# Attention sums in bursts over two shared PSUM banks, with a new order of work, in a four-layer transformer kernel

## The chip, the cores and the metric

One core of one Trainium2 chip. The metric is the device time of one execution in microseconds (us). All runs here are of one core, and "fast" here means within 1.5% of the fastest run of the same kernel. Engines: PE (matmuls), ACT (activations, here the exponentials), DVE (vector work), POOL, and SP (which here only starts DMAs).

## The reference, cut to what matters

The program is four residual layers: linear attention (A), softmax attention (B), A, B. The input has 2048 tokens of width 1024, 32 heads of 32.

```python
def _A_ref(x, wqkv, w_phi, wo):          # linear attention
    q, k, v = ...                        # x @ wqkv
    pq, pk = q @ w_phi, k @ w_phi        # per head
    phi_q = concat([softmax(pq), softmax(-pq)]); phi_k = ...
    kv = einsum("bhsf,bhsd->bhfd", phi_k, v)     # needs every token
    ...                                  # o = phi_q @ kv / den
    return o @ wo
def _B_ref(x, wqkv, wo):                 # softmax attention
    scores = einsum("bhqd,bhkd->bhqk", q, k) * Dh ** -0.5
    p = softmax(scores)
    return (p @ v) @ wo
x = A_x
x = x + _A_ref(layernorm(x), ...)
x = x + _B_ref(layernorm(x), ...)
x = x + _A_ref(layernorm(x), ...)
x = x + _B_ref(layernorm(x), ...)
```

Two things follow. The two softmax layers need 2 x 32 x 2048 x 2048 exponentials. And `kv` in layer A needs every token, so the second A layer can't finish before the first B layer has.

## The kernel before

The kernel is a program that writes a program: while it is built it keeps a clock of its own with a cost for each operation, and it decides from that clock which instruction comes next on each engine. The program that it writes has a fixed order on each engine. Attention is cut into 1024 steps, in the main of two heads x two tiles of 128 keys x 512 queries: 4 QK matmuls (row tiles), 2 exps of 128x1024, and for each exp a group of 4 matmuls of sums (column tiles: values and row sums of both heads). An E tile holds what one exp puts out until its sums have read it. A unit is a run of such steps that adds up in one bank. Everything else (projections with their blocks of weights, the "slabs", the A layers, norms) is "background": tasks that are slipped in between the steps, if their inputs and a PSUM bank are there.

The kernel divides PSUM into eight banks: six are three double-bank `ring` tiles for QK results, one (`acc`) is for sums, one (`bg`) for background.

```python
ring_t = [pps.tile([P, 2, C], F32, ...) for i in range(3)]
acc_t = pps.tile([P, C], F32, tag="acc", name="acc")
bg_t = pps.tile([P, C], F32, tag="bg", name="bg")
# ... cut ...
def exp_chain(u, kks, e, buf):
    E = yield ("take", e_s)                  # 5 E tiles
    yield ("op", "S", c_act(2 * n), lambda x: nc.scalar.activation(
        out=E[:, :, 0:n], in_=ring_t[buf][:, :, 0:n], func=ACT.Exp, scale=INV_SQRT_DH))
    ring.give(buf)
    sums.append((u, kks, e, E))

def emit_sums():                             # sums of an exp as soon as it is there
    while sums:
        u, kks, e, E = sums[0]
        if u.nsum == 0 and not acc_s.free:
            return
        sums.pop(0)
        if u.nsum == 0:
            u.acc = acc_s.take()             # held until the unit's last sum is added
        # ... cut: 4 matmuls into u.acc per 512 columns of E ...
        clk.at(st["t"], lambda E=E: e_s.give(E))
        if final:
            clk.start(finish_unit(u), st["t"] + PE_LAT)      # DVE takes acc out

def get_bank():                              # for a background task
    if bg_free[0]:
        bg_free[0] = False
        # ...
        return bg_t, rel
    if att_active():
        return None                          # ring halves only while no attention runs
    # ... cut: halves of the ring ...

while True:                                  # the order on PE
    # ... cut ...
    if ready and len(ring.free) >= 2:
        emit_step()                          # QK of the next step
        # ... cut ...
        emit_sums()
        continue
    # ... cut: sums, then one background matmul, then wait ...
```

In attention a background "matmul" of 128x512 is written as four column-tiled matmuls ("a group"), so that PE needn't change the tiling mode (row tiles for QK, column tiles for sums; in the trace, at full clock, a group after a group starts 0.216 us later, a QK after a group 0.322 us later); outside attention it is one full-width matmul.

The first layer's tiles are loaded and normalised only when the slot for their transposed chunk is free:

```python
def first_x():
    for t in range(NT):
        u = (0, "K", t // 4)
        yield ("key", ("xs", u))             # the slot
        xb = yield from grab(t_x)
        clk.start(first_x1(u, t, xb))        # load, statistics, normalise
```

The softmax here doesn't subtract the row's maximum and nothing guards it: scores larger than these inputs give would overflow.

Of the kernel before, what the change touches and what calls it, by code (L numbers as in the profile page):

```python
# [35 lines left out]
RATE = {"D": 200e3, "P": 150e3}  # L36
# [181 lines left out]
class Task:  # L218
# [18 lines left out]
    (0, 4, (0,), False, False, (0, 1)), (0, 4, (1,), True, False, (0, 1)), (0, 4, (0, 1), False, False, (2, 3)),  # L237
    (4, 4, (0, 1), False, False, (0, 1, 2, 3, 4, 5, 6, 7)), (0, 4, (0, 1), False, False, (6, 7)),
    (0, 4, (0, 1), False, False, (4, 5)), (8, 4, (0, 1, 2), False, False, (4, 5)),
    (8, 4, (0, 1, 2), False, False, (6, 7)), (0, 4, (2, 3), True, True, (0, 1, 2)),  # L240
    (0, 4, (2, 3), True, True, (3, 4, 5)), (0, 4, (2, 3), True, True, (6, 7)),
    (4, 4, (2, 3), True, True, (6, 7)), (4, 4, (2, 3), True, True, (0, 1, 2, 4, 5)),
    (8, 4, (3,), True, True, (4, 5)), (4, 4, (2, 3), True, True, (3,)),
    (8, 4, (0, 1, 2, 3), False, True, (0, 1)), (8, 4, (0, 1), False, False, (2, 3)),
    (8, 4, (2, 3), True, True, (2, 3)), (8, 4, (3,), True, True, (6, 7)),
    (12, 2, (0, 1, 2, 3), False, True, (6, 7)), (12, 2, (0, 1, 2, 3), False, True, (0, 1, 2, 3, 4, 5)),
    (14, 2, (0, 1, 2, 3), False, True, (0, 3, 6, 7)), (14, 2, (0, 1, 2, 3), False, True, (4, 5)),
    (14, 2, (0, 1, 2, 3), False, True, (1, 2)),
)
VIS3 = (  # L250
    (0, 4, (0,), False, False, (0, 1, 2, 3, 4, 5)), (0, 4, (0,), False, False, (6, 7)),
    (0, 4, (1,), True, False, (0, 1)), (0, 4, (1,), True, False, (2, 3)),
    (4, 4, (0, 1), False, False, (0, 1, 2, 3, 4, 5)), (0, 4, (1,), True, False, (4, 5)),
    (0, 4, (1,), True, False, (6, 7)), (4, 4, (0, 1), False, False, (6, 7)), (0, 4, (2,), True, False, (0, 1)),
    (8, 4, (0, 1, 2), False, False, (0, 1, 2, 3)), (0, 4, (2,), True, False, (2, 3)),
    (8, 4, (0, 1, 2), False, False, (4, 5, 6, 7)), (0, 4, (3,), True, True, (0, 1)),
    (0, 4, (3,), True, True, (2, 3)), (0, 4, (2,), True, False, (4, 5)), (4, 4, (2, 3), True, True, (2, 3)),
    (4, 4, (2, 3), True, True, (0, 1)), (0, 4, (2,), True, False, (6, 7)), (0, 4, (3,), True, True, (4, 5)),
    (0, 4, (3,), True, True, (6, 7)), (4, 4, (2, 3), True, True, (6, 7)), (4, 4, (2, 3), True, True, (4, 5)),
    (12, 2, (0, 1, 2, 3), False, True, (0, 1, 2, 3, 4, 5)), (14, 2, (0, 1, 2, 3), False, True, (1, 2, 4, 5)),  # L260
    (8, 4, (3,), True, True, (0, 1, 2, 3, 4, 5, 6, 7)), (14, 2, (0, 1, 2, 3), False, True, (3,)),
    (14, 2, (0, 1, 2, 3), False, True, (0,)), (12, 2, (0, 1, 2, 3), False, True, (6, 7)),
    (14, 2, (0, 1, 2, 3), False, True, (6, 7)),
# [4 lines left out]
    ('AK', 0, 1, (0, 1), (0,)), ('AK', 0, 0, (0,), (0,)), ('fold', ('pk', 1)), ('AK', 0, 2, (1,), (0,)),  # L268
    ('fold', ('pk', 0)), ('AK', 0, 1, (0, 1), (1,)), ('AO', 0, 0), ('fold', ('pq', 1)),
    ('AK', 0, 0, (0, 1), (1,)), ('AK', 0, 0, (1,), (0,)), ('DN', 0, 0), ('AK', 0, 2, (0,), (1,)),  # L270
    ('AK', 0, 2, (1,), (1,)), ('AK', 0, 3, (0,), (1,)), ('fold', ('pq', 0)), ('AK', 0, 2, (0,), (0,)),
    ('AK', 0, 3, (1,), (0,)), ('DN', 0, 1), ('AO', 0, 1), ('AK', 0, 3, (1,), (1,)), ('AK', 0, 3, (0,), (0,)),
    ('PQ', 0, 1), ('PQ', 0, 0), ('DN', 0, 2), ('PQ', 0, 2), ('BP', 1, 0, (0, 1, 2)), ('BP', 1, 1, (0, 1)),
    ('BP', 1, 2, (0, 1)), ('BP', 1, 1, (2, 3)), ('BP', 1, 0, (3,)), ('PQ', 0, 3), ('AO', 0, 2), ('DN', 0, 3),
    ('BP', 1, 2, (2,)), ('BP', 1, 2, (3,)), ('AO', 0, 3), ('BP', 1, 3, (0, 1)), ('BP', 1, 3, (2,)),
    ('BP', 1, 3, (3,)), ('AK', 2, 0, (0,), (0,)), ('AK', 2, 0, (1,), (0,)), ('BO', 1, 1, 4), ('BO', 1, 8, 10),
    ('PS', 2, 0), ('BO', 1, 11, 13), ('BO', 1, 4, 8), ('BO', 1, 10, 11), ('AK', 2, 1, (1,), (1,)),
    ('BO', 1, 0, 1), ('PS', 2, 1), ('AK', 2, 0, (0, 1), (1,)), ('AK', 2, 2, (0,), (0,)), ('BO', 1, 13, 15),
    ('AK', 2, 2, (1,), (0,)), ('PS', 2, 2), ('BO', 1, 15, 16), ('AK', 2, 1, (0, 1), (0,)),
    ('AK', 2, 1, (0,), (1,)), ('AK', 2, 3, (1,), (0,)), ('AK', 2, 2, (0,), (1,)), ('AO', 2, 0),  # L280
    ('AK', 2, 3, (0,), (0,)), ('AK', 2, 3, (0,), (1,)), ('DN', 2, 1), ('AK', 2, 2, (1,), (1,)),
    ('AK', 2, 3, (1,), (1,)), ('DN', 2, 0), ('PS', 2, 3), ('BP', 3, 0, (0, 1)), ('AO', 2, 1),
    ('BP', 3, 2, (0, 1)), ('AO', 2, 3), ('BP', 3, 0, (2, 3)), ('BP', 3, 2, (2,)), ('BP', 3, 1, (0, 1)),
    ('BP', 3, 2, (3,)), ('DN', 2, 2), ('BP', 3, 3, (0, 1)), ('BP', 3, 1, (2, 3)), ('BO', 3, 12, 14),
    ('AO', 2, 2), ('BO', 3, 15, 16), ('BO', 3, 6, 10), ('DN', 2, 3), ('BO', 3, 14, 15), ('BO', 3, 11, 12),
    ('BO', 3, 0, 2), ('BP', 3, 3, (3,)), ('BP', 3, 3, (2,)), ('BO', 3, 2, 6), ('BO', 3, 10, 11),
# [3 lines left out]
class Unit:  # L290
    def __init__(self, l, vi, qt, w, ks, p, part, last):
        self.l, self.vi, self.qt, self.w, self.ks, self.p = l, vi, qt, w, ks, p
        self.q = qt // 4
        self.n = w * P
        self.g, self.b = divmod(p, 2)
        self.part, self.last = part, last
        kk = [2 * c + m for c in ks for m in range(2)]
        per = 4 // w
        self.steps = [tuple(kk[i:i + per]) for i in range(0, len(kk), per)]
        self.nsum = 0  # L300
        self.acc = None
        self.Q = None
        self.fast = False
# [3 lines left out]
def kernel(  # L307
# [71 lines left out]
    t_x, t_xn, t_phi, t_eq, t_o, t_oT = tok(4), tok(3), tok(8), tok(8), tok(4), tok(4)  # L379
# [4 lines left out]
    acc_t = pps.tile([P, C], F32, tag="acc", name="acc")  # L384
    bg_t = pps.tile([P, C], F32, tag="bg", name="bg")
    ring = Slots(clk, [0, 1, 2])
    acc_s = Slots(clk, [acc_t])
    bg_free = [True]
# [15 lines left out]
    def queue(q, kb):  # L404
        def lat():
            qbusy[q] = max(qbusy[q], clk.now) + kb * 1024 / RATE[q]
            return qbusy[q] - clk.now + DMA_LAT
        return lat
# [7 lines left out]
    def dma_t(o, i):  # L416
        return ("op", "D", 1.3, lambda e: nc.sync.dma_start_transpose(out=o, in_=i), queue("D", 400))
# [123 lines left out]
    def first_x():  # L541
        for t in range(NT):
            u = (0, "K", t // 4)
            yield ("key", ("xs", u))
            xb = yield from grab(t_x)
            clk.start(first_x1(u, t, xb))
# [67 lines left out]
    def slab_plan():  # L614
        want = sorted((slab_next(s), s) for s in slab_use)
        for nxt, s in want[:12]:
            if nxt >= 1 << 30:
                break
# [565 lines left out]
    def finish_unit(u):  # L1184
        token = t_acc
        n = u.n
        if u.part:
            yield ("key", ("pl", u))
            b = part_b.pop(u)
            token = t_part  # L1190
            a = b[:].bitcast(F32)[:, 0:n]
            yield tt("V", c_ps(n), a, a, acc_t[:, 0:n], ALU.add)
        else:
            b = yield from grab(t_acc)
            a = b[:].bitcast(F32)[:, 0:n]
            yield ("op", "V", c_ps(n), lambda e: nc.vector.tensor_copy(out=a, in_=acc_t[:, 0:n]))  # L1196
        acc_s.give(acc_t)
# [132 lines left out]
    sums = []  # L1330
    halves = []
# [65 lines left out]
    def emit_sums():  # L1397
        while sums:
            u, kks, e, E = sums[0]
            if u.nsum == 0 and not acc_s.free:  # L1400
                return
            sums.pop(0)
            if u.nsum == 0:
                u.acc = acc_s.take()
            set_mode("col")
            n = u.n
            n0, d0 = 64 * u.b, 64 * (1 - u.b)
            for i, kk in enumerate(kks):
                c, m = divmod(kk, 2)
                first = u.nsum == 0  # L1410
                u.nsum += 1
                final = u.nsum == 4 * len(u.ks)
                for r0, ld in ((n0, None), (d0, ones)):
                    for j in range(2):
                        h = 2 * u.p + j
                        lh = Vc[c][h // 16][:, 2 * m + e, DH * (h % 16):DH * (h % 16 + 1)] if ld is None else ones[:]
                        nc.tensor.matmul(  # L1417
                            u.acc[r0 + 32 * j:r0 + 32 * j + 32, 0:n], lhsT=lh, rhs=E[:, j, i * n:(i + 1) * n],
                            start=first, stop=final, tile_position=(0, r0 + 32 * j), skip_group_check=True)
                st["t"] += MM * n / C  # L1420
# [150 lines left out]
```

## Time and profile before

| | before |
|---|---|
| time, median of 4 | 2466.0 us |
| profiled span | 2464.0 us |
| ACT busy | 2121 us, 86% |
| exps (2048, starting 904 ns apart in the median) | at least 1851 us |
| time outside attention (before the first exp, gaps of over 2.5 us between exps, after the last) | 517 us |
| attention (the rest) | 1947 us |

The page of the kernel before, its second part: each digit is one of 40 equal slices (61.6 us), the busy share of ACT in tenths, and the granted PE clock in tenths of full speed.

```profile
ACT  4542279996999999999997438999999999999997
PEclk9999999999998899999999999999999995886579
```

ACT is full in two long stretches, the two B layers; where it is not, something else has to be done first. The PE clock is low late in the second.

The same trace by stage (each row a stretch; busy us of each engine and its instructions, PE clock, DMA share, GB/s). The stretches end where exps begin or stop:

```profile
core 0: us, PE busy (x) PEld busy (x) DVE busy (x) ACT busy (x) POOL busy (x), PEclk, DMA share, GB/s
0.00:336.10 336.10, 282.65 (x1983) 151.82 (x1987) 221.30 (x441) 133.21 (x242) 84.61 (x126) 0.98 0.53 161
336.10:578.80 242.70, 231.49 (x3396) 87.68 (x3392) 92.75 (x184) 242.02 (x272) 8.88 (x12) 1.00 0.40 125
578.80:602.90 24.10, 19.40 (x176) 11.72 (x177) 16.18 (x36) 6.02 (x15) 6.37 (x9) 0.93 0.20 53
602.90:1337.70 734.80, 682.68 (x10923) 278.60 (x10915) 420.73 (x674) 728.79 (x816) 127.68 (x141) 0.97 0.35 108
1337.70:1479.40 141.70, 121.50 (x843) 61.89 (x843) 99.59 (x211) 57.17 (x103) 27.15 (x37) 0.99 0.51 146
1479.40:2451.50 972.10, 890.90 (x12231) 325.46 (x12228) 420.54 (x739) 953.90 (x1045) 133.99 (x142) 0.87 0.36 113
2451.50:2464.00 12.50, 7.59 (x40) 3.09 (x39) 5.34 (x7) 0.00 (x0) 0.00 (x0) 0.98 0.11 42
```

Read it like this: rows 2, 4 and 6 are attention with ACT at 98 to 100%. Rows 1, 3, 5 and 7 are the time in which ACT mostly has nothing to do, and in rows 1, 3 and 5 PE works 80 to 86% of the time: what bounds them is projection work on PE and the chains of latency in it. So a change can win by moving background from rows 1, 3 and 5 under the exps, and it can lose by keeping ACT waiting in the others.

And the costliest groups of instructions, from the page: exps, sums, and QK, with the idle time before them:

```profile
L1361 ACT ACTIVATE E<-ring 128x1024 bf16<-128x1024 f32 x2048 | 1905.3, 1183 | 24.8 <-PE ring L1381 24.4
L1417 PE MATMUL acc<-E,V 128*32 128x512 bf16 (+1 forms) x5120 | 694.6, 372 | 2.8 <-ACT E L1361 2.1
...
L1381 PE MATMUL ring<-Q,K2b 32*128 32x512 bf16 (+1 forms) x2560 | 433.0, 364 | 118.2 <-ACT E L1361 110.6
```

PE waited 118 us ahead of one half of the QKs, 111 us of it for an exp to free its ring tile. That is spare time of PE in attention.

### The profile page before, as it was taken

What the parts mean: (1) busy time and instruction counts of PE and PEld (TensorE: products, weight loads), DVE (VectorE), ACT (ScalarE), POOL (GpSimd) and SP (SyncE); (2) the same over time, 40 slices, a digit from 0 to 9 for tenths busy, and PEclk for the clock granted to TensorE, in tenths of its full rate; (3) what the DMA queues carried; (4) which work ended last, traced back from release to release, by engine and by line L of the source; (5) the groups of instructions that cost most, each with busy time, mean ns of one, the idle gap of its engine ahead of it and who ended that gap; (6) DMA issues with size and microseconds to landing.
All of it is one profiled execution on the core that took longest, in us unless ns stands there. A gap on an engine that the chain in (4) does not pass through costs nothing.

```text
span 2464.0 us, 68772 instructions
## 1 busy us (share of the span) xinstructions
PE 2236.2 (91%) x29569; PEld 920.3 (37%) x29569; DVE 1276.4 (52%) x2289; ACT 2121.1 (86%) x2488; POOL 388.7 (16%) x465
## 2 busy tenths in 40 slices
PE   6898899999998989999989889899999989988997
PEld 3444343334332223334444443333333331243233
DVE  6787543244345566476566764534343555432453
ACT  4542279996999999999997438999999999999997
POOL 3321100001011212121114110100020122111120
PEclk9999999999998899999999999999999995886579
DMA  6553563343533332232235445436535353200111
GB/s 223 190 168 83 129 180 108 117 128 106 164 121 121 95 104 89 99 120 52 88 96 189 123 125 159 147 108 195 180 128 149 125 181 124 91 28 19 58 56 40
DMA packets 209906, 296.03 MB, mean 120 GB/s; under 512 B 94656, under 2 KB 113088, under 8 KB 206528
## 3 DMA queue, kind: packets, MB, share of 16 engines
q1 hardware_dynamic: 184512, 185.72, 25.5%
q0 software_dynamic: 25088, 105.92, 12.9%
q8 instruction: 231, 3.78, 0.6%
q14 instruction: 75, 0.61, 0.1%
HBM read 191.95 MB, written 79.69 MB: 110 GB/s over the span
## 4 chain that ended last, share of the span: by engine, by line
PE 46%; ACT 20%; issue 6%; DVE 4%; DMA 1%; ACTq 0%; POOL 0%; DVEq 0%; POOLq 0%
ACT E L1361 18%; PE bg L446 14%; PE acc L1417 14%; PE ring L1381 13%; PE ring L449 3%; DVE blk L432 1%; PE bg L449 1%; DMA xnT<-blk 1%; ACT blk L758 1%; DVE blk L1230 0%; ACT blk L919 0%; DVE blk L1223 0%; DVE sm L799 0%; DMA kvacc<-blk 0%; PE ring L988 0%
## 5 line engine op out<-in xcount | busy, mean ns | idle before, releaser
L1361 ACT ACTIVATE E<-ring 128x1024 bf16<-128x1024 f32 x2048 | 1905.3, 1183 | 24.8 <-PE ring L1381 24.4
L1417 PE MATMUL acc<-E,V 128*32 128x512 bf16 (+1 forms) x5120 | 694.6, 372 | 2.8 <-ACT E L1361 2.1
L1417 PE MATMUL acc<-E,ones 128*32 128x512 bf16 (+1 forms) x5120 | 694.4, 372 | 0.0
L1381 PE MATMUL ring<-Q,K2b 32*128 32x512 bf16 (+1 forms) x2560 | 433.0, 364 | 118.2 <-ACT E L1361 110.6
L1381 PE MATMUL ring<-Q,K2a 32*128 32x512 bf16 (+1 forms) x2560 | 451.7, 366 | 8.5 <-ACT E L1361 8.2
L1417 PEld LDWEIGHTS <-V 128*32 128x32 bf16 x5120 | 199.9, 99 | 298.5 <-issue 271.8
L432 POOL TENSOR_TENSOR blk<-blk,blk 64x512 bf16<-64x512 f32 (+1 forms) x156 | 169.3, 1085 | 713.5 <-DVE blk L1230 573.9
L1381 PEld LDWEIGHTS <-K2a 32*128 32x128 bf16 x2560 | 120.3, 92 | 411.9 <-issue 404.4
L1381 PEld LDWEIGHTS <-K2b 32*128 32x128 bf16 x2560 | 158.9, 92 | 249.5 <-issue 240.1
L1196 DVE COPY blk<-acc 128x512 f32<-128x512 f32 (+1 forms) x160 | 93.3, 583 | 271.9 <-PE acc L1417 271.3
L1230 DVE RECIPROCAL blk<-blk 128x128 f32<-128x128 f32 x252 | 223.8, 923 | 1.8
L1417 PEld LDWEIGHTS <-ones 128*32 128x32 bf16 x5120 | 197.6, 99 | 2.0
L446 PE MATMUL bg<-xnT,slab 128*32 128x512 bf16 x2912 | 192.7, 382 | 5.8 <-DVE K2b L427 2.1
L432 DVE TENSOR_TENSOR blk<-blk,acc 128x512 f32<-128x512 f32 x128 | 87.4, 683 | 172.6 <-PE acc L1417 169.5
L446 PE MATMUL bg<-slab,blk 128*32 128x512 bf16 x2560 | 171.6, 386 | 0.5
L446 PE MATMUL bg<-slab,xnT 128*32 128x512 bf16 (+1 forms) x2496 | 150.2, 361 | 1.6 <-DVE blk L755 0.6
L446 PEld LDWEIGHTS <-slab 128*32 128x32 bf16 x3688 | 101.2, 97 | 104.3 <-issue 21.3
L432 DVE TENSOR_TENSOR blk<-blk,bg 128x512 bf16<-128x512 bf16 x103 | 70.4, 684 | 117.0 <-PE bg L446 113.7
L758 ACT ACTIVATE blk<-ring 128x512 bf16<-128x512 f32 x84 | 47.3, 597 | 97.1 <-PE ring L449 75.9
L449 PEld LDWEIGHTS <-xnT 128*128 128x128 bf16 x792 | 76.8, 98 | 107.4 <-issue 25.7
L427 DVE CAST blk<-bg 128x512 bf16<-128x512 f32 x74 | 51.0, 690 | 123.6 <-PE bg L446 115.9
L446 PEld LDWEIGHTS <-blk 128*32 128x32 bf16 x2904 | 80.2, 98 | 68.9 <-issue 11.8
(184 smaller groups left out, 2281.3 us busy)
## 6 DMA issues: line engine op xcount, KB each, us to landing
slab<-in_B_wqkv_dram POOLq DMA_DIRECT2D x33, 1024.0 KB, 6.6
pd<-blk SPq DMA_DIRECT2D x128, 256.0 KB, 2.3
blk<-pd SPq DMA_DIRECT2D x128, 256.0 KB, 3.5
Q<-qd SPq DMA_DIRECT2D x112, 256.0 KB, 2.8
qd<-blk SPq DMA_DIRECT2D x64, 256.0 KB, 2.6
x<-blk SPq DMA_DIRECT2D x48, 256.0 KB, 2.1
blk<-x SPq DMA_DIRECT2D x48, 256.0 KB, 4.0
slab<-in_A_wqkv_dram POOLq DMA_DIRECT2D x9, 1024.0 KB, 6.6
```

Of the source, the lines that this page charges most:

```text
L427: eng(e).tensor_copy(out=o, in_=i)
L432: return ("op", e, cost, lambda x: eng(x).tensor_tensor(out=o, in0=a, in1=b, op=op))
L446: nc.tensor.matmul(o[js], lhsT=l[:, js], rhs=r, start=st, stop=sp, tile_position=(0, 32 * j), skip_group_check=True)
L449: nc.tensor.matmul(o, lhsT=l, rhs=r, start=st, stop=sp, skip_group_check=True)
L758: yield ("op", "S", c_act(C), lambda x, s=s: nc.scalar.activation(out=e[:, s * C:(s + 1) * C], in_=src, func=ACT.Exp, scale=1.0 - 2.0 * s))
L1196: yield ("op", "V", c_ps(n), lambda e: nc.vector.tensor_copy(out=a, in_=acc_t[:, 0:n]))
L1230: yield ("op", "V", 0.06 + 0.0063 * P, lambda e, x=x: nc.vector.reciprocal(out=r[:, x:x + P], in_=r[:, x:x + P]))
L1361: yield ("op", "S", c_act(2 * n), lambda x: nc.scalar.activation(out=E[:, :, 0:n], in_=ring_t[buf][:, :, 0:n], func=ACT.Exp, scale=INV_SQR ...
L1381: nc.tensor.matmul(ring_t[bufs[e]][:, j, i * n:(i + 1) * n], lhsT=K2[e][c][u.g // 4][r, u.g % 4, m, :], rhs=u.Q[r, e, 0:n], start=True, st ...
L1417: nc.tensor.matmul(u.acc[r0 + 32 * j:r0 + 32 * j + 32, 0:n], lhsT=lh, rhs=E[:, j, i * n:(i + 1) * n], start=first, stop=final, tile_positi ...
```

## The change

The intent: sums no longer occupy a bank for the life of a unit. They wait until all exps of a burst (up to four steps, eight E tiles) are there, then run in one go of eight groups and the bank is emptied. Two banks in one pool then serve sums and background alike. E tiles go from 5 to 9 (24 in place of 26 general buffers pay for them). The first layer's tiles are normalised ahead of their slot. The builder's DMA speeds are new, and with all of this the tables that say in which order attention units and background stages come, and which transposes PE does in place of DMA, were tuned anew.

```diff
-acc_t = pps.tile([P, C], F32, tag="acc", name="acc")
-bg_t = pps.tile([P, C], F32, tag="bg", name="bg")
+work_t = [pps.tile([P, C], F32, tag=f"work{i}", name=f"work{i}") for i in range(2)]
@@ first_x
-            yield ("key", ("xs", u))
@@ finish
-    def finish_unit(u):
+    def finish_burst(u, bank, first, final):
-            yield tt("V", c_ps(n), a, a, acc_t[:, 0:n], ALU.add)
+        if u.part or not first:
+            yield tt("V", c_ps(n), a, a, bank[:, 0:n], ALU.add)
+        work.append(bank)
+        if not final:
+            return
@@ sums
-    def emit_sums():
+    def start_burst():
+        if cur_u[0] is not None or not sums or not work:
+            return
+        u = sums[0][0]
+        need = u.bursts[0]
+        if len(sums) < need or sums[need - 1][0] is not u:
+            return
+        # ... cut: the buffer for the result ...
+        u.acc = work.pop(0)
+        cur_u[0] = u
+    def emit_sum():                      # one E tile's sums; after the last of a burst: finish_burst
@@ get_bank
-        if bg_free[0]:
+        if work:
+            bank = work.pop(0)
@@ main loop
         if ready and len(ring.free) >= 2:
             emit_step()
-            clk.run_until(st["t"])
-            emit_sums()
             continue
+        start_burst()
+        if cur_u[0] is not None:
+            emit_sum()
+            continue
@@ constants
-RATE = {"D": 200e3, "P": 150e3}
+RATE = {"D": 230e3, "P": 230e3}
-NBLK = 26
+NBLK = 24
-TR = {(0, 'K', 0), (0, 'K', 1), (2, 'K', 1), (2, 'O', 0), (2, 'O', 3)}
-NE = 5
+TR = {(0, 'K', 0), (0, 'K', 1), (0, 'O', 2), (1, 'B', 0), (2, 'O', 0), (3, 'B', 0)}
+NE = 9
+BURST = 4
# cut: new tables VIS1, VIS3 (attention units) and STAGES (background)
# cut: buffers for normalised tiles 3 -> 4; two DMA queues slow each other in the builder's clock;
#      HORIZON = 200: a slab is not fetched more than 200 background tasks ahead
```

## The prediction

> **What bounds it now.** The page gives ACT 2121 us of 2464 (86%); its exp group alone is 2048 instructions. Read in the timeline, two exps start 904 ns apart (median), so 2048 x 0.904 = 1851 us is a floor that this change doesn't touch. In the stretches with attention ACT is 98-100% busy; the table by stretch shows it idle elsewhere. The ACT timeline gives these stretches without exps: 336 us before the first exp; 23 us extra after exp 256; 141 us extra after exp 1024 (between the two attention layers), then 8 us; 12.5 us after the last. Sum about 520 us; attention itself takes about 1944. So time is won only by getting projection work out of those 520 us and under the exps, where PE has room: step by step (QK, sums, background groups of four column-tiled matmuls) PE's shortest intervals fit 0.44 us for QK with its two mode switches plus 0.216 us per sum or background group. [...]
>
> **Why room is unused.** One PSUM bank holds a unit's sums for its whole life, one serves background; a background task is 8 groups (1.73 us), then its bank waits for an eviction (DVE cast 0.69 us plus hand-overs). Before, a dense step has 3-4 background groups and PE work of about 50 of 58 us per 32 steps.
>
> **What the change does, by the order of instructions.** QK, exps and sums keep their numbers. Full-width background matmuls fall from about 1,530 to 1,340; dense steps now carry 4.5-5 background groups. Costed with 0.216 us per 512-column matmul and 0.06 per small one:
> - before the first exp 275 -> 229 us of PE work;
> - stop after step 128: 17 -> 0; new stop after step 12: 25;
> - between the layers 119.5 -> 104.6; small stops after steps 528/532: 8 -> one after step 520: 13;
> - tail 7, same.
> Sum 427 -> 379, about -48 us, all of it on the critical path. The time in these stretches is 1.2 times the PE work (latency of norm, transposes, DMA), so some -55. Transposes of the first chunk of each attention layer go from DMA (9 us seen on the chain) to PE, and first-layer tiles are normalised before their slot is free: perhaps -5 to -10 more.
>
> **What it costs.** Sums wait until all exps of a burst (up to 8 E tiles of 9) are done; ACT then has one spare E tile, 0.9 us, until the first sum returns one. PE work per 32 steps rises to 55-62 us against ACT's 58-65: PE becomes co-critical in some 250 steps, and at half clock (seen late in the trace) it could hold ACT up. I put +5 to +20 us on attention. About 10 more exps of other kinds under attention: +5. More partial-sum additions on DVE: off the path.
>
> **Prediction:** 2415 us, range 2380 to 2455; chances 0.5 faster by over 2%, 0.46 within 2%, 0.04 slower.
>
> **Would show it right:** first exp at 275-290 us (was 336); a stop of 25-32 us after exp 24; gap after exp 1024 of 115-130 (was 141); attention stretches near 1950-1965 in total; waits of ACT's exps on PE sums and of sums on ACT small. The wait of PE's QK on exps (119 us before) should fall.
>
> **Would make it wrong:** first exp later than 300 (then a latency chain, not PE work, bounds the start); ACT busy falling below 97% in attention with exps waiting for sums (burst coupling too tight); a granted clock well under 0.93; slabs arriving late, since the order assumes faster DMA.

## More of the kernel before

Whether ACT waits in attention is read from the waits of ACT (who waited for whom, us in total, times, longest):

```profile
engine line waited for: us in total, times, longest us
...
ACT E L1361 <- PE ring L1381: 24.4, 32, 1.9
```

The exps waited 24 us in all for QK results.

## The result

| | before | changed |
|---|---|---|
| time, median of 4 | 2466.0 us | 2421.3 us |
| profiled span | 2464.0 | 2417.6 |
| first exp at | 336.1 | 262.5 |
| stops in layer 1 (gap between exps) | 22.9 | 24.2 |
| between the B layers | 140.3 | 114.3 |
| small stop after it | 5.1 | 12.7 |
| after the last exp | 12.5 | 13.0 |
| outside attention, sum | 517 | 427 |
| attention | 1947 | 1991 |
| ACT idle before exps, in attention | 20 | 48 |
| time at half PE clock | 327 | 426 |

The ratio is 0.9821, 95% interval 0.9804 to 0.9838. Ratios in this text are the mean time of one kernel's fast runs over that of the other's of the same rounds, so not quite the ratio of the medians.

So 90 us left the time outside attention, and 44 came back inside it. The page of the changed kernel (ACT and PE clock in 40 slices of 60.4 us):

```profile
ACT  4542699999999999999995489999999999999997
PEclk9999999999999699999999999899998576678887
```

By stage, as before:

```profile
core 0: us, PE busy (x) PEld busy (x) DVE busy (x) ACT busy (x) POOL busy (x), PEclk, DMA share, GB/s
0.00:262.50 262.50, 229.12 (x1657) 127.26 (x1687) 191.56 (x375) 119.34 (x215) 66.30 (x101) 0.99 0.52 166
262.50:283.50 21.00, 20.99 (x330) 8.05 (x333) 12.82 (x24) 20.98 (x24) 1.29 (x2) 1.00 0.56 152
283.50:308.90 25.40, 25.19 (x186) 14.34 (x184) 11.57 (x26) 8.83 (x22) 5.46 (x8) 1.00 0.85 218
308.90:1278.30 969.40, 910.46 (x14992) 386.17 (x14988) 562.85 (x965) 956.62 (x1072) 169.42 (x200) 0.96 0.43 134
1278.30:1393.70 115.40, 105.11 (x862) 59.25 (x871) 92.60 (x195) 53.76 (x99) 31.68 (x44) 0.97 0.53 172
1393.70:2404.70 1011.00, 879.74 (x12258) 339.74 (x12249) 430.07 (x751) 965.19 (x1057) 133.18 (x145) 0.84 0.35 107
2404.70:2417.60 12.90, 7.54 (x39) 3.09 (x39) 5.35 (x7) 0.00 (x0) 0.00 (x0) 0.99 0.11 41
```

The first row is 74 us shorter, with PE busy 87% of it (84% before). The fifth row is 26 us shorter. But the sixth, the second attention layer, is 1011 us for 1057 ACT instructions, where the kernel before took 972 us for 1045: ACT is busy 95% of it (98% before), and the clock is 0.84 (0.87).

The waits of ACT in the changed kernel:

```profile
engine line waited for: us in total, times, longest us
...
ACT E L1365 <- PE ring L1385: 48.5, 118, 2.3
...
ACT E L1365 <- PE work L1439: 4.2, 8, 1.3
```

Exps now wait 48.5 us, twice as long, 118 times in place of 32, and for QK. For an E tile that sums hold (the second line) they wait only 4.2 us.

The groups of the changed kernel that answer to those shown before:

```profile
L1365 ACT ACTIVATE E<-ring 128x1024 bf16<-128x1024 f32 x2048 | 1910.7, 1124 | 54.1 <-PE ring L1385 48.5
L1439 PE MATMUL work<-E,V 128*32 128x512 bf16 (+1 forms) x5120 | 641.5, 387 | 7.0 <-DVE blk L438 4.4
...
L1385 PE MATMUL ring<-Q,K2b 32*128 32x512 bf16 (+1 forms) x2560 | 438.4, 369 | 123.2 <-ACT E L1365 118.1
```

**Where in attention the time went.** In the trace, the ACT idle time just before exps (gaps under 2.5 us) was sorted by whether the PE clock was half for over 1 us of the preceding 2 us. Before: 12.7 us at half clock, 10.7 at full. Changed: 40.9 at half, 10.2 at full. (The 20 and 48 us of the table leave out the first exp after each stop.) The whole growth is in half-clock stretches, above all in the last quarter of the attention steps (the second half of the second B layer), where little background is left: there exps wait 28.3 us in the changed kernel (from 1870 us on) and 5.0 in the kernel before (from 1924 us on).

The idle time is not all of the 44 us. ACT's idle time in attention grew from 21 to 50 us and its busy time by 15 us, from 1926 to 1941: 13 more instructions other than exps (94, not 81) run there, and the exps themselves are busy 1911 us in place of 1905.

A stretch of the timeline of the kernel before in such a place, at half clock (start, length, engine, instruction; lines for the row sums, which start 0.01 us or less after the value sums, are left out):

```profile
start us, us, engine line op out<-in xcount [idle before <-releaser]
2059.55 11.30 ACT L1361 ACTIVATE E<-ring 128x1024 bf16<-128x1024 f32 x12
...
2061.63 0.61 PE L1381 MATMUL ring<-Q,K2b 32*128 32x512 bf16 x2
...
2062.16 0.61 PE L1417 MATMUL acc<-E,V 128*32 128x512 bf16 x2
...
2062.57 0.64 PE L1417 MATMUL acc<-E,V 128*32 128x512 bf16 x2
...
2062.99 0.64 PE L1417 MATMUL acc<-E,V 128*32 128x512 bf16 x2
...
2063.57 0.61 PE L1381 MATMUL ring<-Q,K2a 32*128 32x512 bf16 x2
```

Three groups of sums, 0.42 us each, lie between two QKs: QK to QK is 1.94 us, and the next interval, with one group, is 1.1 us; ACT runs through (12 exps in a row). The changed kernel in the same situation:

```profile
start us, us, engine line op out<-in xcount [idle before <-releaser]
1904.40 2.85 ACT L1365 ACTIVATE E<-ring 128x1024 bf16<-128x1024 f32 x3
1904.56 0.61 PE L1385 MATMUL ring<-Q,K2b 32*128 32x512 bf16 x2 [0.74 <-ACT E L1365]
1905.10 0.61 PE L1439 MATMUL work<-E,V 128*32 128x512 bf16 x2
...
1905.50 0.64 PE L1439 MATMUL work<-E,V 128*32 128x512 bf16 x2
...
1905.92 0.64 PE L1439 MATMUL work<-E,V 128*32 128x512 bf16 x2
...
1906.35 0.64 PE L1439 MATMUL work<-E,V 128*32 128x512 bf16 x2
...
1906.92 0.61 PE L1385 MATMUL ring<-Q,K2a 32*128 32x512 bf16 x2
...
1907.63 3.77 ACT L1365 ACTIVATE E<-ring 128x1024 bf16<-128x1024 f32 x4 [0.38 <-PE ring L1385]
```

Four groups stand between the QKs. From the QK at 1904.56 to the next at 1906.92 are 2.36 us; two exps take 1.81. The ring holds one step and a half, so ACT runs dry at 1907.25 and waits 0.38 us for QK. At full clock the same four groups take about 0.87 us (4 x 0.216), and exps waited no longer than before. And just before, ahead of the QK at 1904.56, PE itself had waited 0.74 us for ACT: on average it has time enough, only the work comes in lumps.

In the clock records of the two traces only the values 0.5 and 1.0 occur. There are 35 half-clock stretches in the kernel before and 66 in the changed one. All but the last of each (2.6 and 2.3 us, at the end of the trace) last 3.4 us or a whole multiple of it: 18 and 42 of them last 3.4 us, the others 6.8, 10.2 and so on up to 71.7 us (before) and 37.5 us (changed).

### The profile page after: what moved, and what is told of

It is laid out like the page before. It is cut to its first block, busy times and chain, and to the rows that moved or that the text cites. A ratio compares the mean times of both kernels' runs of the same rounds, so it can differ in the third digit from the quotient of the medians.

```text
span 2417.6 us, 70484 instructions
## 1 busy us (share of the span) xinstructions
PE 2178.1 (90%) x30290; PEld 937.9 (39%) x30334; DVE 1306.8 (54%) x2341; ACT 2124.7 (88%) x2482; POOL 407.3 (17%) x500
## 4 chain that ended last, share of the span: by engine, by line
PE 74%; ACT 15%; issue 5%; DVE 4%; DMA 1%; POOL 0%; SPq 0%; ACTq 0%; another core or an unknown queue 0%; DVEq 0%; POOLq 0%
PE work L452 24%; PE work L1439 20%; PE ring L1385 16%; ACT E L1365 13%; PE work L455 9%; PE ring L455 3%; DVE blk L438 2%; ACT blk L763 1%; PE work L838 1%; DMA kvacc<-blk 1%; PE work L993 0%; DVE sm L804 0%; DMA slab<-in_A_wqkv_dram 0%; PE ring L838 0%; DVE blk L1233 0%
## 5 line engine op out<-in xcount | busy, mean ns | idle before, releaser
L1365 ACT ACTIVATE E<-ring 128x1024 bf16<-128x1024 f32 x2048 | 1910.7, 1124 | 54.1 <-PE ring L1385 48.5
L1439 PE MATMUL work<-E,V 128*32 128x512 bf16 (+1 forms) x5120 | 641.5, 387 | 7.0 <-DVE blk L438 4.4
L1439 PE MATMUL work<-E,ones 128*32 128x512 bf16 (+1 forms) x5120 | 641.4, 387 | 0.0
L1385 PE MATMUL ring<-Q,K2a 32*128 32x512 bf16 (+1 forms) x2560 | 441.5, 371 | 48.5 <-ACT E L1365 48.4
L438 DVE TENSOR_TENSOR blk<-blk,work 128x512 f32<-128x512 f32 (+1 forms) x289 | 196.0, 680 | 413.8 <-PE work L1439 352.6
L1439 PEld LDWEIGHTS <-V 128*32 128x32 bf16 x5120 | 253.4, 106 | 235.3 <-issue 155.7
L1197 DVE COPY blk<-work 128x512 f32<-128x512 f32 (+1 forms) x160 | 93.4, 584 | 361.4 <-PE work L1439 359.4
L452 PE MATMUL work<-slab,blk 128*32 128x512 bf16 x2768 | 180.2, 382 | 1.0 <-DVE blk L438 0.9
L452 PE MATMUL work<-slab,xnT 128*32 128x512 bf16 (+1 forms) x2208 | 134.2, 368 | 2.5 <-DVE blk L438 1.2
L452 PE MATMUL work<-xnT,slab 128*32 128x512 bf16 x2048 | 136.0, 385 | 0.1
L455 PE MATMUL work<-slab,xnT 128*128 128x512 bf16 (+1 forms) x524 | 115.4, 372 | 2.6 <-DMA slab<-in_A_wqkv_dram 1.7
L438 POOL TENSOR_TENSOR blk<-blk 128x256 bf16<-128x256 f32 x95 | 68.4, 731 | 200.6 <-DVE blk L438 166.4
```

The costliest lines, as they stand in the source:

```text
L438: return ("op", e, cost, lambda x: eng(x).tensor_tensor(out=o, in0=a, in1=b, op=op))
L452: nc.tensor.matmul(o[js], lhsT=l[:, js], rhs=r, start=st, stop=sp, tile_position=(0, 32 * j), skip_group_check=True)
L455: nc.tensor.matmul(o, lhsT=l, rhs=r, start=st, stop=sp, skip_group_check=True)
L1197: yield ("op", "V", c_ps(n), lambda e: nc.vector.tensor_copy(out=a, in_=bank[:, 0:n]))
L1385: nc.tensor.matmul(ring_t[bufs[e]][:, j, i * n:(i + 1) * n], lhsT=K2[e][c][u.g // 4][r, u.g % 4, m, :], rhs=u.Q[r, e, 0:n], start=True, st ...
L1439: nc.tensor.matmul(u.acc[r0 + 32 * j:r0 + 32 * j + 32, 0:n], lhsT=lh, rhs=E[:, j, i * n:(i + 1) * n], start=u.first, stop=end, tile_positi ...
```

## The experiments

Builds of the same kernels with one part changed. In the expectations "exposed" time is the time outside attention, the "prefix" is what comes before the first exp, and s is one group of sums. "Exps wait" is the ACT idle before exps in attention; "outside" and "attention" are as above. All were correct.

| run | ratio to before [95%] | median us | first exp | outside | attention | exps wait | half clock |
|---|---|---|---|---|---|---|---|
| (before) | 1 | 2466.0 | 336 | 517 | 1947 | 20 | 327 |
| (changed) | 0.9821 [0.9804, 0.9838] | 2421.3 | 263 | 427 | 1991 | 48 | 426 |
| late_smooth | 0.9692 [0.9667, 0.9717] | 2388.8 | 264 | 428 | 1957 | 24 | 480 |
| warm | 0.9676 [0.9651, 0.9701] | 2384.9 | 264 | 436 | 1950 | 19 | 72 |
| late_and_warm | 0.9704 [0.9686, 0.9722] | 2393.9 | 264 | 434 | 1961 | 28 | 125 |
| before_warm | 0.9968 [0.9945, 0.9990] | 2459.3 | 337 | 523 | 1935 | 13 | 60 |
| code_only | 1.0284 [1.0249, 1.0318] | 2532.1 | 345 | 506 | 2021 | 76 | 557 |
| code_old_dma | 1.0150 [1.0135, 1.0165] | 2503.2 | 311 | 482 | 2015 | 73 | 506 |
| code_old_dma_warm | 0.9929 [0.9909, 0.9950] | 2448.8 | 311 | 485 | 1957 | 31 | 69 |
| order_only | 1.0509 [1.0482, 1.0536] | 2591.1 | 291 | 612 | 1973 | 41 | 484 |
| one_bank_each | 1.0837 [1.0821, 1.0853] | 2672.5 | 285 | 667 | 2003 | 64 | 507 |
| not_ahead | 1.0150 [1.0133, 1.0167] | 2500.9 | 289 | 481 | 2011 | 64 | 488 |
| smooth_and_warm | 0.9819 [0.9802, 0.9836] | 2420.7 | 261 | 448 | 1967 | 33 | 131 |

One warning for all of them: the builder re-plans every later instruction when a rule changes. Only `late_smooth`, `late_and_warm`, `warm`, `before_warm` and `code_old_dma_warm` keep the background work and the stops of the kernel they start from (by the order of instructions, within 1 us of PE work, though in the traces the four with dummies have one or two new gaps of 2.7 to 6.6 us between exps; `late_smooth` is the same instruction for instruction up to row 48,893 of 60,671 on PE). The others move several things at once, and their totals are read with that in mind.

### late_smooth: the lumps taken away, in the last quarter only

```diff
+    # U_LATE = 216: from about step 728 of 1024; cut: start_burst(True) doesn't ask for a full burst
+        if sums and cur_u[0] is None and sums[0][0].l == 3 and st["ui"] >= U_LATE:
+            start_burst(True)        # begin with one exp done, when no background can run
+            if cur_u[0] is not None:
+                continue
```

> Edit: the changed kernel, but in the last quarter of the second attention layer (from about step 728 of 1024) a burst of sums may start as soon as one exp is done, when nothing in the background can run. By the order of instructions all PE work up to there and all stops without attention are the same; after it the sums come as QK ss QK ss instead of QK QK ssss QK ssss. Theory A (lumps of four sums between two QKs[...] starve ACT): of the 27 us that ACT idles before exps between 1850 us and the end, fewer than 6 stay, the time falls by 20 to 27 us to about 2395 to 2401, ratio to the kernel before about 0.972, with the clock still half for much of that stretch. Rival B (the half clock alone or DVE or DMA holds exps up, not the bursts): idle time and total stay within 5 us, ratio 0.982.

(The low clock itself is measured: 0.73 in the changed kernel from 1870 us to the last exp. Theory A is about lumps of sums at that clock.)

Measured: 2388.8 us, ratio 0.9692. That is 32 us less than the changed kernel, more than the 20 to 27 of theory A, and the clock in this stretch fell further. (Step 728 lies in the middle of the second attention layer: "last quarter" is true of all 1024 steps.) The last quarter by stage, first the changed kernel, then this run:

```profile
core 0: us, PE busy (x) PEld busy (x) DVE busy (x) ACT busy (x) POOL busy (x), PEclk, DMA share, GB/s
1870.00:2404.70 534.70, 430.73 (x5688) 161.88 (x5685) 194.08 (x296) 505.83 (x543) 73.94 (x70) 0.73 0.20 65
```

```profile
1870.00:2371.80 501.80, 488.54 (x5682) 162.72 (x5681) 192.35 (x295) 497.70 (x543) 74.36 (x70) 0.64 0.21 69
```

The waits of the exps in the same two stretches, again the changed kernel first:

```profile
ACT E L1365 <- PE ring L1385: 28.3, 78, 1.0
ACT E L1365 <- PE ring L1385: 4.1, 3, 1.7
```

The same 543 ACT instructions and nearly the same PE instructions take 501.8 us in place of 534.7, at a clock of 0.64 in place of 0.73. Of 28.3 us of waits 4.1 stay (theory A: fewer than 6). The other 8 us or so are busy time of ACT (497.7 in place of 505.8 for the same instructions); why the exps are busy for less was not followed up. So neither the half clock alone nor DVE or DMA held the exps up. It was the lumps. Rival B falls.

### warm: the lumps kept, the half clock taken away

```diff
+        if work and cur_u[0] is None and st["t"] - st["last"] < 3.0 and clk.heap and clk.heap[0][0] > st["t"] + 0.05:
+            set_mode("col")
+            for j in range(4):       # ones x identity into a free bank, never read
+                nc.tensor.matmul(work[-1][32 * j:32 * j + 32, :]..., lhsT=ones[:], rhs=ident[:]..., start=True, stop=True, ...)
+            st["t"] += MM
+            continue
```

> Edit: the changed kernel, with dummy column-tiled matmuls of constants into a free bank, never read, wherever PE would idle in attention between bursts (about 1330 groups); bursts, stops and tables are as in the changed kernel. Theory A (burst lumps hurt only at half clock): half-clock time falls from 425 us to under 100, and the ACT idle before exps of about 48 us in attention falls to 10 to 20; time about 2390 to 2402, unless dummies delay QK. Rival C (burst lumps starve ACT at any clock, since QK has only one and a half steps of ring ahead): clock up, but idle stays above 35 us and the time stays within 8 us of 2421.

Measured: 2384.9 us, ratio 0.9676; 72 us at half clock; exps wait 19 us. The same last quarter:

```profile
1870.00:2371.80 501.80, 501.72 (x9380) 225.30 (x9380) 194.79 (x297) 501.69 (x548) 74.34 (x70) 1.00 0.22 72
```

The clock is 1.00, ACT is busy 501.7 of 501.8 us with no wait of an exp left, and the stretch has the very length of `late_smooth`. The bursts are nearly as they were: between two QKs lie four or more groups of sums 419 times in the trace of the changed kernel and 406 times here. (One gap of 6.6 us without exps in layer 1, which the changed kernel did not have, is new here; it is counted as outside.) So lumps starve ACT only at half clock: rival C falls.

### late_and_warm: are these one loss or two?

Both edits together.

> Edit: the changed kernel with both remedies, without the reordering in layer 1 that the run smooth_and_warm had (there new waits of 10 us on a DMA transpose and a longer middle stop came in): early start of bursts in the last quarter of layer 2, dummy matmuls elsewhere. If both remedies act on one loss (lumps at half clock): no better than the better one, 2378 to 2390, ratio 0.965 to 0.969, ACT idle before exps 12 to 22 us. If two losses: 2350 to 2365.

Measured: 2393.9 us, ratio 0.9704: the two don't add. The time and the 28 us of waits are above the ranges for one loss (2378 to 2390, 12 to 22 us), and far above the time for two. The traces of the single remedies say more: in the last quarter `late_smooth` takes the waits from 28 to 4 us and `warm` to none, and elsewhere both leave the 20 us or so of the changed kernel. So it is one loss, and either remedy takes it back. That the sum is a little worse than each alone (by 5 to 9 us, with 11 us of exps waiting in the last quarter again) was not followed up.

### before_warm: does a full clock help by itself?

The dummy matmuls in the kernel before, into its background bank.

> Edit: the kernel before with dummy matmuls of constants into the background bank where PE would idle in attention; tables and stops as before. A control for the run warm, which won 36 us. If the half clock costs time only where the sums come in lumps (theory A): half-clock time falls from 327 us to under 120 and the time stays within 0.5% (2455 to 2478). If a full clock helps any kernel by itself: 2430 to 2445, as in warm.

Measured: 2459.3 us, ratio 0.9968: half clock fell from 327 to 60 us and the time by 0.3%. Attention became 12 us shorter (1935 in place of 1947), and two new gaps of 3.1 and 2.7 us took part of it back; in `warm` attention became 41 us shorter. The kernel before, whose sums are spread, had little to lose to the half clock. This is the control for `warm`, and it passes.

### code_only and order_only: which half of the change wins?

`code_only` is the changed code with the tables VIS1, VIS3, STAGES and TR of before; `order_only` is the code of before with the changed tables.

> Edit: the changed kernel's code (bursts, two shared banks, 9 E tiles, tiles normalised ahead, DMA model) with the tables of the kernel before (visits, stages, list of PE transposes). By the order of instructions PE work outside attention is about 402 us (273.7 before the first exp, 106 between the layers, one stop of 10, one of 5, tail 7) against 427 before and 379 changed. If the code alone brings the gain: about 2421. My theory (banks and order work only together, and bursts cost some 25 to 30 us of ACT idle at half clock): first exp at 305 to 325 us, middle stop 115 to 125, attention 1960 to 1985, total 2440 to 2465, ratio 0.99 to 1.0.

> Edit: the kernel before, its code untouched, with the changed tables (visits, stages, list of PE transposes). By the order of instructions it starts attention as early as the changed kernel (225 us of PE work) but then stops eleven times more, 505 us of PE work outside attention against 427. If the new order is what brought the gain: 2430 or less. My theory (the order needs the second bank; one background bank cannot deliver in time): about 2530 to 2570, ratio 1.025 to 1.045.

Measured: 2532.1 us (ratio 1.0284) and 2591.1 us (1.0509). Each half alone makes the kernel slower; together they make it 1.8% faster. `order_only` starts attention at 291 us but stops again and again, 612 us outside attention in all. My direction was right, both sizes were too small. For `code_only` the first exp came at 345 us, not at 305 to 325, and there were stops with no PE work in them. In its trace PE waits 12 and 10 us on two DMA-transposed tiles before the first exp, which led to the next run. (All its waits on DMA before the first exp are 25 us, not the 35 that the next expectation names.)

### code_old_dma and code_old_dma_warm: why code_only was so slow

`code_old_dma` gives the builder the DMA speeds of before as well:

```diff
-RATE = {"D": 230e3, "P": 230e3}
+RATE = {"D": 200e3, "P": 150e3}
# and the queue model of before, transposes counted as 400 KB
```

> Edit: as code_only (changed code, tables of before), and the scheduler's DMA speeds are those of before too (200 and 150 GB/s, transposes as 400 KB). PE work outside attention 402 us by the order of instructions. code_only took 2532, with PE waits of 35 us on DMA-transposed tiles and loads before the first exp and some 14 us of new stops with no PE work. If that came of an order that counts on faster DMA with old tables: first exp back at 315 to 335 us, new stops gone, total 2450 to 2490, ratio 0.995 to 1.01. If bursts with the old order cost it: still above 2510.

Measured: 2503.2 us, ratio 1.0150. 29 us came back, the first exp at 311 us, but attention stayed at 2015 us. The total is in neither range (2450 to 2490, or above 2510), and short stops of 3 to 5 us are still there. So an order that counts on faster DMA explains a part. The rest was put to the test with the dummies:

> Edit: as code_old_dma (changed code; tables and DMA speeds of before), plus the dummy matmuls of the run warm. code_old_dma took 2503 us: exposed time 482 us against 517 before, but attention 2015 us against 1947, with 73 us of ACT idle and 506 us at half clock. If those 68 us are lumps at half clock as well: half clock under 120 us, ACT idle 20 to 35, attention 1955 to 1975, total 2440 to 2460, ratio 0.99 to 0.998. If they come from the old order with bursts (late DMA, waits for banks): total above 2485.

Measured: 2448.8 us, ratio 0.9929, attention 1957 us. Another 54 us were lumps at half clock. So with the old order the new code would be worth 0.7% if it did not pay for its lumps; with them it costs 1.5%.

### one_bank_each: is it the sharing?

```diff
-    work = list(work_t)
+    work = [work_t[0]]
+    wbg = [work_t[1]]
@@ get_bank
-        if work:
-            bank = work.pop(0)
+        if wbg:
+            bank = wbg.pop(0)
# cut: and it is given back to wbg
```

> Edit: the changed kernel, tables and bursts kept, but one of the two banks is for sums alone and the other for background alone. By the order of instructions the prefix is the same (229 us of PE work) but ten stops without attention hold 305 us in place of 149. If sharing the two banks is what lets the background keep up: the exposed time grows from 427 us to about 590, the ACT idle at half clock shrinks or stays, total about 2560 to 2610, ratio 1.04 to 1.06. If the order of visits does it and the banks matter little: within 1% of 2421, ratio 0.98 to 0.99.

Measured: 2672.5 us, ratio 1.0837, 667 us outside attention: with these tables, sharing is what lets the background keep up, even more than expected. (Tables tuned for banks of their own were not tried with bursts. The waits of exps, which were to shrink or stay, grew from 48 to 64 us.) And it showed something that I had not counted. Before the first exp:

```profile
core 0: us, PE busy (x) PEld busy (x) DVE busy (x) ACT busy (x) POOL busy (x), PEclk, DMA share, GB/s
0.00:284.50 284.50, 238.30 (x1656) 129.93 (x1683) 194.79 (x374) 120.51 (x216) 66.73 (x101) 0.97 0.50 153
```

The PE work is the same (1656 matmuls, 1657 in the changed kernel), yet it takes 284.5 us in place of 262.5, with PE idle 46 us in place of 33; the other 9 us are busy time, at a clock of 0.97 in place of 0.99. Where no attention runs, the pool gives background a bank that before the change lay unused.

### not_ahead: normalising ahead undone

```diff
         for t in range(NT):
             u = (0, "K", t // 4)
+            yield ("key", ("xs", u))
```

(and three buffers in place of four for normalised tiles).

> Edit: the changed kernel, but the first layer's tiles wait for their slot before they are loaded and normalised (and 3 in place of 4 buffers for normalised tiles), as before the change. By the order of instructions PE work before the first exp is 241 us in place of 229, in all outside attention 397 in place of 379. If normalising ahead is what took the prefix's PE idle from 53 us to 33: first exp at 285 to 300 us, total 2440 to 2460, ratio about 0.993. If the idle went for other reasons (tables, DMA model, one more bank): first exp at 272 to 280, total about 2430 to 2440, ratio about 0.987.

Measured: 2500.9 us, ratio 1.0150, first exp at 288.9 us. The start came out as the first alternative said:

```profile
0.00:288.90 288.90, 244.92 (x1721) 134.54 (x1753) 203.82 (x396) 120.82 (x218) 70.52 (x109) 0.97 0.57 168
```

PE idles 44 us here, 33 in the changed kernel; the other 16 us are busy time of PE, most of it extra work that the builder put ahead of the first exp (12 us by the order of instructions). The total missed my figure by 40 us and more: the re-planned order had a new stop of 30 us after exp 464 and 20 us more in attention. So the total says nothing about normalising ahead; the first 289 us do.

### smooth_and_warm: a failed combination

As `late_and_warm`, with early starts also in units 64 to 91 of layer 1.

> Edit: the changed kernel with both remedies: bursts may start early in the last quarter of layer 2 and in units 64 to 91 of layer 1, and dummy matmuls where PE would idle between bursts. If both remedies act on the same loss (ACT idle from four-sum lumps at half clock), they do not add: 2375 to 2388, ratio 0.964 to 0.969, ACT idle before exps 8 to 20 us. If they are two losses: 2350 to 2360.

Measured: 2420.7 us, ratio 0.9819, in neither range. The early starts in layer 1 re-planned what follows: PE waits 10 us on one DMA transpose, the middle stop is 128 us in place of 114, and exps wait 13.5 us for E tiles. It can't tell the theories apart; `late_and_warm` was run in its place.

## Why the prediction was right, and where it wasn't

The time is inside the range, 6 us from the figure predicted. The likeliest of the three classes in the prediction was "faster by over 2%", at 0.5; the measured 1.8% is in the class that had 0.46. But two terms of the sum were off, in opposite directions: the time outside attention fell by 90 us where 60 to 65 were predicted, and attention grew by 44 where 10 to 25 were. That the sum came out so near is partly luck.

- **PE work moved from outside attention under the exps (-48 us): right.** In the traces PE is busy 435 us outside attention before and 377 after, 58 less. The term was counted from the order of instructions and costed from the trace, and `order_only`, `code_only` and `one_bank_each` show that neither the order nor the banks bring it alone (each with tables that were tuned for the other kernel or its banks).
- **Latency outside attention: mis-sized.** The prediction had "some -55" and "perhaps -5 to -10 more"; the measured change is -90. It let the time per PE work stay at 1.2; in the traces it fell from 1.19 to 1.13 of PE's busy time, as PE's idle time outside attention fell from 82 to 50 us. Before the first exp it fell from 53 to 33 us, because of the second bank that background has there (`one_bank_each`: 22 us later with the same work) and normalising ahead (`not_ahead`: PE idles 11 us more). Hence the first exp at 262.5 and not at 275 to 290. The middle stop was 114.3, at the edge of 115 to 130. In the chain of work that ended last there the kernel before has a DMA transpose of 9.3 us and the changed kernel has no DMA left, which agrees with the move of transposes to PE; what that alone is worth no run shows.
- **Cost in attention: mis-sized, and the mechanism named first was not the one.** The prediction put "+5 to +20 us on attention" and +5 for other exps; measured are +44, 29 of it idle time of ACT and 15 busy time. It named E tiles: one spare tile until the first sum returns one. The trace has only 4.2 us of that. What it has is 48.5 us of exps waiting for QK, since in the last quarter mostly four groups of sums or more stand between two QKs and at half clock take longer than the exps. That PE "at half clock (seen late in the trace) ... could hold ACT up" was the right side remark; `late_smooth`, `warm` and `before_warm` show it, and that either cure brings 32 to 36 us back. One sign named under "Would make it wrong" came half true: ACT fell to 95% busy in the second B layer, but with exps waiting for QK, not for sums.
- **PE co-critical in dense steps: not seen.** At full clock exps waited 10.2 us (10.7 before). The fuller PE that the prediction estimated (55 to 62 us per 32 steps) did no harm there. One saving was not counted: with sums in bursts, the order of instructions has 1823 changes of PE's tiling mode in place of 2153. At some 0.11 us each (worked out in the last section) that is an estimated 36 us of PE time. It fits that PE's busy time in attention is 1801 us in both traces, though background came in.
- **"The wait of PE's QK on exps should fall": wrong.** Over both halves of QK it rose from 119 to 167 us. The idle time of PE in attention grew from 145 to 190 us, about as much as attention itself. It is unevenly spread: in the timeline at 1904 us shown above PE waits 0.74 us for ACT before four groups of sums, and ACT 0.38 us for PE after them.
- **Granted clock "well under 0.93": partly.** It was 0.912 as a mean. The mean doesn't tell what it costs: `late_smooth` has 0.90 and is 32 us faster.

What stays open: how much the PE transposes alone are worth (the changed kernel with only the old list of transposes could not be built: the builder found no task that it could place), why the two remedies together are slightly worse than each alone, and where the 20 us of waits come from that neither remedy touches. Best of all kernels here is `warm`, 2384.9 us, 3.2% under the kernel before; `late_smooth`, which needs no dummy work, is within its interval.

## What to carry to other kernels

When work is batched to free a resource sooner, ask what now stands in front of the instruction that feeds the bottleneck engine, at the worst speed of the engine that runs it: an engine that has time to spare in sum (here PE, busy 431 of 535 us in the last quarter) can still starve the next one, if the queue between them is shorter than one lump (here, at half clock, 2.36 us from QK to QK against 1.81 us for two exps). Batch where the resource is wanted, and go back to small pieces where it isn't. And a tuned order and the buffers it was tuned for are one thing: tested apart, each half of this change was slower than the original.

## What the traces show of the PE clock and the tiling mode

- The half clock came without long gaps of PE. It was half for 327 us (before) and 426 us (changed), while from the middle of the trace on the longest PE gap in such a stretch, or in the 7 us ahead of it, was 1.9 us in both. Nor did a PE that is busy nearly all the time keep it full: in the last quarter of `late_smooth` PE is busy 488.5 of 501.8 us in the trace, at a mean clock of 0.64. How much work keeps the full clock these runs don't show. With dummies in the gaps the mean clock was 0.985 (`warm`; 0.912 in the changed kernel) and 0.988 (`before_warm`; 0.934 in the profiled run of the kernel before).
- Matmuls of constants were enough for that: the dummies were ones times identity, and with them the half-clock time fell from 426 to 72 us (`warm`) and from 327 to 60 us (`before_warm`).
- A half clock was nearly free in two places. In `late_smooth` the clock was 0.64 over 501.8 us with ACT 99% busy, and `warm` took as long for the same stretch at 1.00; in the kernel before, taking most of it away brought 0.3%.
- A change of the tiling mode took time on PE. In both traces, at full clock, a group of four column-tiled matmuls of 512 columns starts 0.216 us after one like it (median), but a QK of as many columns starts 0.32 us after such a group, and such a group 0.32 us after a QK. So an estimated 0.11 us a change, and some 0.43 us for a QK with both of its changes (the prediction has 0.44).
